# Turning the local attention's weights as two halves of 64 rows, with a PSUM bank for each half

## The chip, the cores and the metric

The kernel runs on one core of one Trainium2 chip. The metric is the device time of one execution in microseconds (us). The time before is the median of three runs, 1090.08 us (1089.24 to 1092.59).

## What is computed

Two kinds of attention are added, and the sum goes through a layer norm and a two-layer network with a residual. In the shapes of this case there are 8 batches, 8 heads, 576 positions and a head size of 64, so 4608 rows of 512 numbers reach the network, all in float32.

```python
# local attention: each position sees the 7 positions around it
mask = np.abs(pos[:, None] - pos[None, :]) < 4
scores = np.where(mask, scale * np.matmul(q, k.transpose(0, 1, 3, 2)), -1e9)
out_local = softmax(scores) @ v
# pooled attention: q, k and v averaged over groups of 4 positions
out_up = np.repeat(softmax(scale * q_d @ k_d.T) @ v_d, 4, axis=2)
x = (out_up + out_local) laid out as (8, 576, 512)
xn = (x - mean) / np.sqrt(var + 1e-6) * g_ln
return x + np.maximum(xn @ w_ch1, 0.0) @ w_ch2      # 512 -> 2048 -> 512
```

## The kernel before

**The work and its tiles.** The local attention is cut into 40 windows, five for each batch. A window holds two blocks of 64 positions and all 8 heads, so its tiles have 128 rows. The pooled attention runs in 16 halves of four heads. The network takes the 4608 rows in 18 chunks of 256 (two tiles of 128 rows each); in each chunk there are 8 steps `p` of `up` (line 940, tile `h`) and `down` (line 963, tile `acc`). Both products are made of three products of split float32 numbers, which is why TensorE carries most of the time.

**One window** (`local(i)`), in the order of its data:

- SyncE loads q and k (`qr`, `kr`, line 391: eight loads each, in two groups of four, one group for each half `jb`) and v (`vwin`, line 409, four loads). VectorE turns q and k in blocks of 32 (`lqt`, `lkt`, line 472). In the first seven windows TensorE turns them instead (line 431).
- TensorE makes the scores `ls` (line 513, 32 products of 64x64, each on a quarter of the array). VectorE masks them and subtracts the largest, ScalarE makes the exponentials `la` (line 539), a tile of 128 rows by 8 heads by 64.
- **`turn_a` (line 548) turns `la`**: four transposes of 128x128 on TensorE, one for each pair of heads, into one PSUM bank `lt`. **`turn_a_out` (line 555)** copies that bank to SBUF on ScalarE as `at`, one instruction of 128x512.
- `times_v` (line 569) multiplies by v: 32 products of 64x64 by 64x65 into two banks `lv`. It reads rows 0 to 63 of `at` for one set of products and rows 64 to 127 for the other, in all columns.
- VectorE divides (`xl`, line 585; sometimes ScalarE, line 588), and SyncE moves the rows of `xl` to the tiles `x` of the network (line 628).

**From a window to the network** (`norm(n)`): SyncE loads the pooled result `up` (line 831), GpSimd adds it to `x` (line 855), VectorE makes the statistics `st` and `mv` (line 859), GpSimd the root, VectorE the normed tile `xn` (line 869), and TensorE turns it (`px`, line 879) for the chunk that follows. Tile n needs the last of the windows that overlap it: tile 27 needs window 31, and tile 29 needs window 33.

**What sets the order.** All steps are tasks of a `Plan`. Each task names an engine, a length, the tasks that it needs, a due time, and the rooms that it takes and gives: 87 buffers in SBUF (`u`), eight PSUM banks (`a`), two staging buffers. `order()` goes through an imagined time and picks on each engine the task with the earliest due time among those that can start. That order is then the program's order on every engine, SyncE's queue of loads among them, and each engine keeps it: an instruction that waits holds all that stands behind it on its engine. A task with `alt` may go to a second engine, whichever starts sooner. So a new length or a new room of one task can move other tasks, on any engine.

Of the kernel before, what the change touches and what calls it, by code (L numbers as in the profile page):

```python
# [22 lines left out]
class Plan:  # L23
# [14 lines left out]
    def add(self, eng, dur, fn, deps=(), due=0.0, take=(), give=(), lag=None, ahead=1e9, alt=None, kb=0):  # L38

        opts = {eng: (dur, fn, 0.0)}  # L40
        if alt is not None:
            opts[alt[0]] = alt[1:]
        t = SimpleNamespace(
            n=len(self.tasks), opts=opts, dur=dur, deps=[d for d in deps if d is not None],
            due=due, take=take, give=give, lag=lag, ahead=ahead, open=0.0, waits=0, eng=None, fn=None, kb=kb,
        )
        self.tasks.append(t)
        return t
# [91 lines left out]
def attention_then_ffn(  # L140
# [10 lines left out]
    nc = tc.nc  # L151

    P = 128
# [17 lines left out]
    NPAIR = H // 2  # L171
# [15 lines left out]
    def unit(shape, name, dtype=F32, kind="u"):  # L187
        kind = kind if kind in SEP else "u"
        return work.tile(shape, dtype, tag=kind, bufs=SEP.get(kind, NU), name=name)

    def psa(name):
        return ps_a.tile([P, 512], F32, tag="a", name=name)
# [9 lines left out]
    ident = const.tile([P, P], F32, name="ident")  # L202
# [64 lines left out]
    def window_at(i):  # L267
        if NWIN <= i < NWIN + NEARLY:
            return w_base + i * w_gap - EARLY
        return w_base + i * w_gap if i >= NWIN else norm_at(0) - B0W - B0W_GAP * (2 - i)  # L270
# [21 lines left out]
    U, A, STG = (("u", 1),), (("a", 1),), (("stg", 1),)  # L292
    DMA, LAT, W_AHEAD = 0.5, 2.9, 40

    def act(n, sbuf=False):
        return (0.155 if sbuf else 0.14) + n / 1430.0

    def dve(n):
        return 0.06 + n / 950.0
# [72 lines left out]
    def window_start(w, par):  # L372
        return min(max(NQ * (2 * w + par) - (FACTOR - 1), 0), S - 64)

    last_local = SimpleNamespace(v=[None, None])

    def local(i):
        b, w = divmod(i, NWIN)
        due = window_at(i)
        add = plan.add  # L380
        x = SimpleNamespace(r={}, p={}, raw={})
# [14 lines left out]
        def load_rows(src, nm):  # L396
            x.raw[nm] = unit([P, H, D], f"{nm}n{i}")
            for par in range(2):
                t0 = window_start(w, par)
                nc.sync.dma_start(  # L400
                    x.raw[nm][64 * par : 64 * par + 64], src[b, :, t0 : t0 + 64, :].rearrange("h c d -> c h d")
                )
# [20 lines left out]
        for src, nm in ((q, "q"), (k, "k")):  # L423
            if by_pe:
# [16 lines left out]
                def sums(nm=nm):  # L441

                    for par in range(2):
# [16 lines left out]
                t = add("SP", 1.46, lambda src=src, nm=nm: load_rows(src, nm), (), due - 12.0, take=U,  # L460
                        lag=LAT, kb=256, ahead=AHEAD)
                t = add("PE", 0.43, turn, (t,), due - 8.0, take=A, give=U)
                if own:
                    t = add("DVE", 4 * dve(120), sums, [t] + gsum_done.get((b, nm), []), due - 8.0,
                            take=() if w else (("u", 2),))
# [16 lines left out]
        vt = add("SP", 4 * DMA, load_v, (last_local.v[i % 2],), due - 8.0, lag=LAT, kb=256, ahead=AHEAD)  # L482
# [35 lines left out]
        def masked(n):  # L518
            nc.vector.tensor_add(x.ps[n], x.ps[n], mask.unsqueeze(1).broadcast_to([P, NPAIR, 64]))
# [23 lines left out]
                    nc.scalar.activation(a[:, pr], x.ps[h2][:, pr], AF.Exp, scale=SCALE, bias=x.mx[:, n : n + 1])  # L543

        def turn_a():
            x.pt = psa(f"lt{i}")
            for pr in range(NPAIR):
                nc.tensor.transpose(  # L548
                    x.pt[:, pr * P : (pr + 1) * P],
                    x.a[:, 2 * pr : 2 * pr + 2].rearrange("p h j -> p (h j)"), ident,  # L550
                )

        def turn_a_out():
            x.at = unit([P, NPAIR, P], f"at{i}")
            nc.scalar.copy(x.at.rearrange("p h j -> p (h j)"), x.pt)

        def times_v():

# [14 lines left out]
        def inverse(h2):  # L573
            r = work.tile([P, NPAIR], F32, tag="lr", bufs=8, name=f"lr{i}_{h2}")
            nc.vector.tensor_scalar_add(r, x.pv[h2][:, :, D], 1e-9)
            nc.vector.reciprocal(r, r)
            x.r[h2] = r

        def divided(h2, eng):
            if h2 == 0:  # L580
                x.xl = unit([P, H, D], f"xl{i}")
            xl = x.xl.rearrange("p (c h) d -> p h c d", h=2)[:, h2]
            pv, r = x.pv[h2], x.r[h2]
            if eng == "DVE":
                nc.vector.tensor_mul(xl, pv[:, :, :D], r.unsqueeze(2).broadcast_to([P, NPAIR, D]))
                return
            for pr in range(NPAIR):
                nc.scalar.activation(xl[:, pr], pv[:, pr, :D], AF.Copy, scale=r[:, pr : pr + 1])

        by_dve = i in SHIFTED or i >= LATE  # L590
        t = add("PE", 0.75, scores_by_pair if by_pe else scores_by_block, turned, due - 6.0,
                take=(("a", 2),), give=(("u", 2),))
        if not by_pe:
            t = add("DVE", dve(256), lambda: masked(0), (t,), due - 5.0)
            t = add("DVE", dve(256), lambda: masked(1), (t,), due - 5.0)
        t = add("DVE", 2 * dve(256) + (2 * dve(256) if by_dve else 0.15), largest_by_pair, (t,), due - 5.0)
        t = add("ACT", 2 * act(256) if by_dve else 1.6, exps_by_pair, (t,), due - 5.0, take=U, give=(("a", 2),))
        t = add("PE", 0.43, turn_a, (t,), due - 3.0, take=A, give=U)
        at = add("ACT", act(512), turn_a_out, (t,), due - 3.0, take=U, give=A)
        last_local.v[i % 2] = tv = add("PE", 0.7, times_v, (at, vt), due - 1.0, take=(("a", 2),), give=U)  # L600
        outs = []
        for h2 in range(2):
            t = add("DVE", 0.28, lambda h2=h2: inverse(h2), (tv,), due)
            outs.append(
                add("DVE", dve(256), lambda h2=h2: divided(h2, "DVE"), [t] + outs, due, take=() if h2 else U, give=A,
                    alt=("ACT", 4 * act(64), lambda h2=h2: divided(h2, "ACT"), 0))
            )
        moves = []
        for par in range(2):
            s0 = NQ * (2 * w + par)  # L610
            n = min(NQ, S - s0)
            t, r0 = b * S + s0, s0 - window_start(w, par)
            while n:
                m = min(n, P - t % P)
                moves.append((t // P, t % P, r0, m, par))
                t, r0, n = t + m, r0 + m, n - m
        for e, (n, p0, r0, m, par) in enumerate(moves):

            def move(n=n, p0=p0, r0=r0, m=m, par=par):
# [7 lines left out]
                for h2 in range(2):  # L627
# [5 lines left out]
            t = add("SP", DMA if by_pe else 2 * DMA, move, outs, due + 1.0, take=() if n in piece else U,  # L633
                    give=U if e == len(moves) - 1 else (), lag=LAT, kb=116)
# [370 lines left out]
    for i in range(NPB * NWIN):  # L1005
        local(i)
    for b in range(B):
        pooled(b)
    for i in range(NPB * NWIN, B * NWIN):
        local(i)  # L1010
# [42 lines left out]
```

## Time and profile before

| | |
|---|---|
| median of three runs | 1090.08 us |
| the profiled execution's own time | 1095.81 us |
| its span, first to last instruction | 1092.7 us |
| TensorE busy (matmul) | 1040.4 us, 95% |
| VectorE, ScalarE, GpSimd busy | 504.5, 311.0, 268.8 us |
| mean granted TensorE clock | 0.973 |

The profile records one execution, so all durations come from an execution that took 5.73 us more than the median of the runs. PE is TensorE's matmul row and PEld its weight loads, DVE is VectorE, ACT ScalarE, POOL GpSimd, SP SyncE. A timeline's row gives the start in us, the time that the group of like instructions covers, the engine and line, the operation, its tiles and shapes, and how often; in brackets stands the idle time ahead of it and what ended it. Matmul rows overlap, since they are pipelined: what a group takes from the others is read from starts, not from durations. A row of the windows gives, for each engine, the busy time and in brackets the number of instructions that run in that stretch, those included that began ahead of it; then the granted clock.

### The profile page before, as it was taken

The numbers are of one execution on the slowest core, as the hardware profiler recorded it, in microseconds if no ns is written. First come the engines' busy times: TensorE is split into PE (matmuls) and PEld (weight loads), VectorE is DVE, ScalarE is ACT, GpSimd is POOL, SyncE is SP. The second block draws the span as 40 slices with busy tenths as digits, with TensorE's granted clock in tenths as the row PEclk, the third lists the DMA queues.
The fourth block names the chain that finished last, engine by engine and source line by source line (L and its number), as shares of the span: only waits on it lengthen the run. The fifth ranks groups of instructions, "written<-read, shape, count | busy, mean of one in ns | idle before, by whom it ended". The sixth has DMA issues, their size and how long they took to land.

```text
span 1092.7 us, 23624 instructions
## 1 busy us (share of the span) xinstructions
PE 1040.4 (95%) x9182; PEld 929.1 (85%) x9182; DVE 504.5 (46%) x1305; ACT 311.0 (28%) x852; POOL 268.8 (25%) x277
## 2 busy tenths in 40 slices
PE   7879889989999999999999999999988999999998
PEld 6768778878989898899898889898977989888997
DVE  7579863624344443453533443544424353543211
ACT  5366542313322222131322132223212222212100
POOL 2224556322202440041323231132400230100000
PEclk9679899999999999999999999999998999999999
DMA  7589845533433543325353534244433243320000
GB/s 147 130 227 269 214 126 125 137 75 82 103 72 80 113 101 70 90 62 122 71 119 74 123 74 113 43 113 90 116 68 76 62 98 62 81 53 29 9 20 19
DMA packets 289885, 105.38 MB, mean 96 GB/s; under 512 B 238022, under 2 KB 276166, under 8 KB 289774
## 3 DMA queue, kind: packets, MB, share of 16 engines
q1 hardware_dynamic: 289774, 103.88, 40.9%
q8 instruction: 72, 1.18, 0.5%
q14 instruction: 39, 0.32, 0.1%
HBM read 82.58 MB, written 11.80 MB: 86 GB/s over the span
## 4 chain that ended last, share of the span: by engine, by line
PE 72%; DMA 10%; SPq 7%; DVE 5%; issue 3%; POOL 3%; ACT 1%; DVEq 0%; POOLq 0%; ACTq 0%
PE h L940 30%; PE acc L963 29%; DMA x<-xl 4%; PE gv L768 2%; SPq L628 2%; PE lv L569 2%; PE gs L732 2%; PE ls L513 2%; DMA s<-in_moe_w_ch_dram 2%; DVE cva L343 1%; PE lt L548 1%; SPq L391 1%; PE px L879 1%; SPq L409 1%; PE gt L751 1%
## 5 line engine op out<-in xcount | busy, mean ns | idle before, releaser
L963 PE MATMUL acc<-hi,hl 128*128 128x512 f32 x576 | 239.5, 416 | 5.5 <-DVE hl L951 5.5
L963 PE MATMUL acc<-lo,hh 128*128 128x512 f32 x576 | 229.7, 399 | 0.0
L963 PE MATMUL acc<-hi,hh 128*128 128x512 f32 x576 | 227.6, 395 | 0.0
L947 ACT ACTIVATE hh<-h 128x512 fp32r<-128x512 f32 x144 | 86.3, 599 | 429.5 <-PE h L940 374.2
L951 DVE SCALAR_TENSOR_TENSOR hl<-h,hh 128x512 fp32r<-128x512 f32 x144 | 98.7, 685 | 216.3 <-ACT hh L947 201.4
L940 PE MATMUL h<-xh,lo 128*128 128x256 f32 x1152 | 192.9, 290 | 0.3 <-POOL lo L356 0.3
L940 PE MATMUL h<-xlo,hi 128*128 128x256 f32 x1152 | 185.6, 283 | 0.0
L940 PE MATMUL h<-xh,hi 128*128 128x256 f32 x1152 | 184.8, 283 | 0.0
L940 PEld LDWEIGHTS h<-xh,lo 128*128 128x128 f32 x1152 | 168.7, 189 | 17.7 <-POOL lo L356 0.6
L940 PEld LDWEIGHTS h<-xlo,hi 128*128 128x128 f32 x1152 | 159.0, 192 | 0.4
L940 PEld LDWEIGHTS h<-xh,hi 128*128 128x128 f32 x1152 | 158.3, 191 | 0.0
L855 POOL TENSOR_TENSOR x<-x,up 128x512 f32<-128x512 f32 x32 | 41.1, 1286 | 429.9 <-DMA x<-xl 266.5
L963 PEld LDWEIGHTS acc<-hi,hh 128*128 128x128 f32 x576 | 109.9, 191 | 25.4
L963 PEld LDWEIGHTS acc<-hi,hl 128*128 128x128 f32 x576 | 110.5, 192 | 22.6 <-DVE hl L951 6.5
L963 PEld LDWEIGHTS acc<-lo,hh 128*128 128x128 f32 x576 | 110.8, 192 | 13.0
L886 ACT ACTIVATE xh<-px,gain 128x128 fp32r<-128x128 f32 x144 | 43.6, 371 | 87.1 <-PE px L879 58.1
L859 DVE BATCH_NORM_STATS2 st<-x 128x6 f32<-128x512 f32 x36 | 24.8, 690 | 83.9 <-POOL x L855 83.8
L896 DVE SCALAR_TENSOR_TENSOR xlo<-px,gain,xh 128x128 fp32r<-128x128 f32 x144 | 42.4, 342 | 35.7 <-ACT xh L886 31.5
L343 DVE SCALAR_TENSOR_TENSOR cva<-s,cva 128x256 int32<-128x256 int32 x64 | 42.0, 697 | 1.1
L745 ACT ACTIVATE ag<-gs,gmx 96x144 f32<-96x144 f32 x96 | 29.0, 372 | 45.7 <-DVE gmx L737 42.5
L768 PEld LDWEIGHTS gv<-vd,agt 72*72 72x72 f32 x512 | 39.1, 151 | 2.4 <-POOL vd L680 0.8
L768 PE MATMUL gv<-vd,agt 72*72 72x65 f32 x512 | 40.0, 234 | 0.9 <-POOL vd L680 0.7
(176 smaller groups left out, 1101.4 us busy)
## 6 DMA issues: line engine op xcount, KB each, us to landing
s<-in_moe_w_ch_dram SPq DMA_DIRECT2D x64, 256.0 KB
vwin<-in_v_dram SPq DMA_DIRECT2D x160, 64.0 KB
out_dram<-x SPq DMA_DIRECT2D x36, 256.0 KB
qr<-in_q_dram SPq DMA_DIRECT2D x264, 32.0 KB
kr<-in_k_dram SPq DMA_DIRECT2D x264, 32.0 KB
up<-ud SPq DMA_DIRECT2D x28, 256.0 KB
x<-xl SPq DMA_DIRECT2D x66, 58.0 KB
ud<-od SPq DMA_DIRECT2D x32, 72.0 KB
```

What stands on the lines that cost most here:

```text
L343: nc.vector.scalar_tensor_tensor(out=a, in0=x.raw[i].rearrange("p (n two) -> p n two", two=2)[:, :, 0], scalar=29, in1=a, op0=ALU.logical_ ...
L513: nc.tensor.matmul(x.ps[par][64 * h2 : 64 * h2 + 64, pr], lhsT=x.qt[hs, 2 * pr + h2], rhs=x.kt[hs, 2 * pr + h2], start=True, stop=True,)
L745: nc.scalar.activation(y.a[:, c], y.ps[:, c], AF.Exp, scale=POOLED_SCALE, bias=y.mx[:, c : c + 1])
L768: nc.tensor.matmul(y.pv[:, qh, h2], lhsT=y.at[kh][:, h2, qh * GH : (qh + 1) * GH], rhs=vd[:, kh, 2 * pr + h2], start=kh == 0, stop=kh == 1,)
L855: (nc.vector if by_pe else nc.gpsimd).tensor_add(xt[n], xt[n], x.up)
L859: nc.vector.bn_stats(st, xt[n])
L886: nc.scalar.activation(xh[c][i][:, k, j * P : (j + 1) * P], pxt[n][:, kc], AF.Copy, scale=gain[:, kc : kc + 1])
L896: nc.vector.scalar_tensor_tensor(out=xlo[c][i][:, k, ts], in0=pxt[n][:, kc], scalar=gain[:, kc : kc + 1], in1=xh[c][i][:, k, ts].bitcast(F ...
L940: nc.tensor.matmul(ph[c, p][:, fi], lhsT=wt[:, kc], rhs=xx[kc // 2][:, kc % 2], start=n == 0, stop=n == 3 * KC - 1)
L947: nc.scalar.activation(hh[c, p], ph[c, p], AF.Relu)
L951: nc.vector.scalar_tensor_tensor(out=hl[c, p].rearrange("p c t -> p (c t)"), in0=ph[c, p].rearrange("p c t -> p (c t)"), scalar=0.0, in1=h ...
L963: nc.tensor.matmul(acc[c][j], lhsT=lt[:, fi, ts], rhs=rt, start=p == 0 and fi == 0 and n == 0, stop=p == NPR - 1 and fi == 1 and n == 2,)
```

## The change

The transposes of `la` are cut in two halves of 64 rows. For each pair of heads there are two transposes, of rows 0 to 63 and of rows 64 to 127, each with the fitting 64x64 corner of the identity, and each half has a PSUM bank of its own. So four transposes of 128x128 become eight with 128 columns of the stationary operand and 64 of the moving one. The copy to SBUF is cut likewise: each half's bank is copied into its 64 columns of every pair, and the plan may put each copy on ScalarE or VectorE. In the plan, `turn_a` takes two banks in place of one, its length is 0.27 in place of 0.43, and each copy gives one bank back.

```diff
         def turn_a():
-            x.pt = psa(f"lt{i}")
+
+            x.pt = [psa(f"lt{i}_{n}")[:, : NPAIR * 64].rearrange("p (c j) -> p c j", c=NPAIR) for n in range(2)]
             for pr in range(NPAIR):
-                nc.tensor.transpose(
-                    x.pt[:, pr * P : (pr + 1) * P],
-                    x.a[:, 2 * pr : 2 * pr + 2].rearrange("p h j -> p (h j)"), ident,
-                )
-
-        def turn_a_out():
-            x.at = unit([P, NPAIR, P], f"at{i}")
-            nc.scalar.copy(x.at.rearrange("p h j -> p (h j)"), x.pt)
+                for n in range(2):
+                    hs = slice(64 * n, 64 * n + 64)
+                    nc.tensor.transpose(
+                        x.pt[n][:, pr], x.a[hs, 2 * pr : 2 * pr + 2].rearrange("p h j -> p (h j)"), ident[hs, hs],
+                    )
+
+        def turn_a_out(n, copy):
+            if n == 0:
+                x.at = unit([P, NPAIR, P], f"at{i}")
+            copy(x.at[:, :, 64 * n : 64 * n + 64], x.pt[n])
...
-        t = add("PE", 0.43, turn_a, (t,), due - 3.0, take=A, give=U)
-        at = add("ACT", act(512), turn_a_out, (t,), due - 3.0, take=U, give=A)
-        last_local.v[i % 2] = tv = add("PE", 0.7, times_v, (at, vt), due - 1.0, take=(("a", 2),), give=U)
+        t = add("PE", 0.27, turn_a, (t,), due - 3.0, take=(("a", 2),), give=U)
+        at = []
+        for n in range(2):
+            at.append(add("ACT", act(256), lambda n=n: turn_a_out(n, nc.scalar.copy), [t] + at, due - 3.0,
+                          take=() if n else U, give=A,
+                          alt=("DVE", dve(256), lambda n=n: turn_a_out(n, nc.vector.tensor_copy), 0.1)))
+        last_local.v[i % 2] = tv = add("PE", 0.7, times_v, at + [vt], due - 1.0, take=(("a", 2),), give=U)
```

The lines behind the change stand three to seven higher in the changed kernel (line 940 is 947 there).

TensorE at window 23, in the middle of the program, before; the number in a name is that of the window, chunk or tile:

```order
L751 MATMUL gt10_1_0_7736<-ident_66,ag10_1_7720 72x96 x3
L751 MATMUL gt10_1_1_7742<-ident_66,ag10_1_7720 72x96 x3
L548 MATMUL lt23_7751<-ident_66,la23_7695 128x128 x4
L940 MATMUL h9_1_7705<-xh9_0_7535,lo1_3_1209 128x256 x2
L940 MATMUL h9_1_7705<-xh9_1_7547,lo1_3_1209 128x256 x2
```

The same place of the changed kernel:

```order
L758 MATMUL gt10_1_0_7891<-ident_66,ag10_1_7835 72x96 x3
L758 MATMUL gt10_1_1_7896<-ident_66,ag10_1_7835 72x96 x3
L551 MATMUL lt23_0_7900<-ident_66,la23_7790 128x64
L551 MATMUL lt23_1_7901<-ident_66,la23_7790 128x64
L551 MATMUL lt23_0_7900<-ident_66,la23_7790 128x64
L551 MATMUL lt23_1_7901<-ident_66,la23_7790 128x64
L551 MATMUL lt23_0_7900<-ident_66,la23_7790 128x64
L551 MATMUL lt23_1_7901<-ident_66,la23_7790 128x64
L551 MATMUL lt23_0_7900<-ident_66,la23_7790 128x64
L551 MATMUL lt23_1_7901<-ident_66,la23_7790 128x64
L947 MATMUL h9_1_7871<-xh9_0_7685,lo1_3_1258 128x256 x2
L947 MATMUL h9_1_7871<-xh9_1_7697,lo1_3_1258 128x256 x2
```

The four full transposes are eight halves, which alternate between the two banks; their neighbours are the same.

SyncE's queue at window 31, before: the loads of k for window 32 (`kr32`) stand between the moves of window 30 and of window 31 to tile 27 (`x27`):

```order
L666 DMA raw14v1_10011<-in_v_dram 72x4x256
L409 DMA vwin0_77<-in_v_dram 64x4x64 x4
L666 DMA raw15q0_10059<-in_q_dram 72x4x256
L628 DMA x27_10064<-xl30_10044 58x4x64 x4
L391 DMA kr32_10096<-in_k_dram 32x8x32 x4
L391 DMA qr33_10129<-in_q_dram 32x8x32 x4
L666 DMA raw15k0_10160<-in_k_dram 72x4x256
L391 DMA kr32_10096<-in_k_dram 32x8x32 x4
L391 DMA qr33_10129<-in_q_dram 32x8x32 x4
L791 DMA ud6_8953<-od13_1_10183 72x2x128
L831 DMA up27_10259<-ud6_8953 128x1x512
L409 DMA vwin1_78<-in_v_dram 64x4x64 x4
```

The same stretch of the changed kernel:

```order
L391 DMA kr32_10177<-in_k_dram 32x8x32 x4
L391 DMA qr32_10131<-in_q_dram 32x8x32 x4
L673 DMA raw14v1_10223<-in_v_dram 72x4x256
L391 DMA kr32_10177<-in_k_dram 32x8x32 x4
L409 DMA vwin0_77<-in_v_dram 64x4x64 x4
L635 DMA x27_10287<-xl30_10247 58x4x64 x4
L391 DMA qr33_10338<-in_q_dram 32x8x32 x4
L673 DMA raw15q0_10356<-in_q_dram 72x4x256
L673 DMA raw15k0_10369<-in_k_dram 72x4x256
L798 DMA ud6_9143<-od13_1_10374 72x2x128
L391 DMA qr33_10338<-in_q_dram 32x8x32 x4
L838 DMA up27_10435<-ud6_9143 128x1x512
```

All eight loads of `kr32` now stand ahead of `vwin0`, so that eight loads fewer lie between window 30's moves and `vwin1`; one load, `raw15q0`, has come in between. `ud6` is no longer right ahead of `up27`, which reads it. In both kernels window 31's moves to tile 27 (two loads of 12x4x64) follow right behind `vwin1`.

VectorE's queue at the normed tile 27, before:

```order
L859 BN_STATS st27_10344<-x27_10064 128x6
L861 BN_AGGR mv27_10346<-st27_10344 128x2
L862 TENSOR_SCALAR mv27_10346<-mv27_10346 128x1
L472 STREAM_TRANSPOSE lkt32_10371<-kr32_10096 128x512
L472 STREAM_TRANSPOSE lqt33_10373<-qr33_10129 128x512
L869 TENSOR_SCALAR xn27_10385<-x27_10064,mv27_10346 128x512
```

And of the changed kernel:

```order
L472 STREAM_TRANSPOSE lqt33_10563<-qr33_10338 128x512
L866 BN_STATS st27_10565<-x27_10287 128x6
L868 BN_AGGR mv27_10567<-st27_10565 128x2
L869 TENSOR_SCALAR mv27_10567<-mv27_10567 128x1
L903 SCALAR_TENSOR_TENSOR xlo13_0_10579<-px26_10541,gain_75,xh13_0_10570 128x128 x2
L876 TENSOR_SCALAR xn27_10593<-x27_10287,mv27_10567 128x512
```

`lkt32` no longer stands between the statistics and `xn27` (it stands 20 rows ahead of the statistics), and `lqt33` has moved ahead of the statistics. Of the 80 copies of `lt` in the changed kernel, 68 stand on ScalarE and 12 on VectorE.

## The prediction, on record ahead of the result

> **What bounds the kernel now.** The page comes first: busy times, the granted clock, the chain that ended last.
>
> ```profile
> span 1092.7 us, 23624 instructions
> PE 1040.4 (95%) x9182; PEld 929.1 (85%) x9182; DVE 504.5 (46%) x1305; ACT 311.0 (28%) x852; POOL 268.8 (25%) x277
> ...
> PEclk9679899999999999999999999999998999999999
> ...
> PE 72%; DMA 10%; SPq 7%; DVE 5%; issue 3%; POOL 3%; ACT 1%; DVEq 0%; POOLq 0%; ACTq 0%
> ```
>
> TensorE is the bound: 95% busy, 72% of the chain, at full clock but for the first quarter and one dip in the 30th slice. So a change counts here by what it adds to TensorE's row of starts, and by what it does to the few places where TensorE stands still. The dip is the largest of these after the start-up. The timeline of TensorE around it, and the windows view of the ten us that follow, show it:
>
> ```profile
> 814.06 0.39 PE L963 MATMUL acc<-hi,hh 128*128 128x512 f32 x1
> 822.83 1.09 PE L879 MATMUL px<-ident,xn 128*128 128x128 f32 x4 [8.38 <-DVE xn L869]
> ...
> 817.00:827.00 10.00, 4.17 (x18) 3.17 (x18) 4.82 (x12) 1.90 (x7) 0.13 (x1) 0.50 0.30 65
> ```
>
> TensorE stood idle for 8.38 us waiting for the normed tile 27, and its clock was 0.50 until about 827, so that the 4.2 us of work from 822.83 on lost another 2.1. This wait cost about 10.5 us. The Trainium skill, "TensorE: Matmul & The Clock Gate", Part 1, says that an idle window of some 3.4 us halves the clock; this row agrees with it.
>
> **The transposes on TensorE.** The groups by line give what is replaced, and a price for a half copy; the tile view from 260 us on gives the count and who waits for the copies.
>
> ```profile
> L548 PE MATMUL lt<-ident,la 128*128 128x128 f32 x160 | 25.1, 280 | 5.8 <-ACT la L543 4.5 <-ACT la L539 1.2
> ...
> L555 ACT COPY at<-lt 128x512 f32<-128x512 f32 x40 | 23.5, 588 | 40.4 <-PE lt L548 36.6 <-issue 2.9 <-DMA out_dram<-x 0.7
> ...
> L539 ACT ACTIVATE la<-ls 128x256 f32<-128x256 f32 x64 | 22.0, 386 | 36.9 <-DVE ls L529 36.7
> ...
> L548 PE MATMUL lt<-ident,la x120: 270/272/328, 277.8 to 1006.9; 128*128 128x128 f32 x120
> ...
>   PEld lv L569: 0.4, 1
> ```
>
> There are 40 groups of four, and 30 of them lie behind 260 us, where TensorE runs without a break and every ns of its row counts. What one group takes is read from starts, in the timeline at window 23:
>
> ```profile
> 605.35 0.60 PE L548 MATMUL lt<-ident,la 128*128 128x128 f32 x4
> ...
> 606.27 0.64 PE L940 MATMUL h<-xh,hi 128*128 128x256 f32 x4
> 606.74 0.64 PE L940 MATMUL h<-xlo,hi 128*128 128x256 f32 x4
> ```
>
> From the transposes' start to the second group of `h` are 0.92 us, and one group of four `h` takes 0.47, so the transposes cost 0.45 us.
>
> No row before has products on half the rows and all columns. The nearest are the products on a quarter of the array, `ls` and `lv`, which also leave the full array and come back to it:
>
> ```profile
> 594.41 0.39 PE L963 MATMUL acc<-lo,hh 128*128 128x512 f32 x1
> 594.64 0.39 PE L963 MATMUL acc<-hi,hh 128*128 128x512 f32 x1
> 594.96 0.69 PE L513 MATMUL ls<-lkt,lqt 64*64 64x64 f32 x32
> ...
> 596.15 0.64 PE L940 MATMUL h<-xh,hi 128*128 128x256 f32 x4
> ```
>
> One `acc` takes 0.23, so a plain successor would have started at 594.87; `ls` started at 594.96, 0.09 late. From there to the second group of `h` are 1.19, less 0.47 is 0.72. So the 32 products cost 0.81 us. The windows view of the same group says how much of that is work:
>
> ```profile
> 595.06:595.41 0.35, 0.35 (x28) 1.00 0.39 61
> 594.95:595.06 0.11, 0.11 (x5) 1.00 0.42 64
> ```
>
> Up to 595.06 there run the last `acc` and the first round of four products; in the next 0.35 us these four and 24 more, which is six rounds at 0.058 us. Eight rounds are 0.46, and 0.35 us are left for going in and out. A half transpose streams 64 columns as one `ls` does, and two halves use disjoint rows and two banks, so I take four rounds of 0.058, 0.23 us, and the same 0.35: 0.58 us. That is 0.13 more than now. From both sides: without any cost of entry the group would be cheaper (the second rival); the first weight load has 128 columns in place of 64, which may add 0.05, and a round might be 0.01 dearer. So 0.11 to 0.19 where the entry is paid.
>
> The Trainium skill, "TensorEngine Tiling (Array Packing)", Key Properties, says that a change of tiling mode drains TensorE, and it lists 64x128 as a mode of its own. Of the 64x64 mode the rows above agree, with 0.35 us a visit; of 64x128 no run here shows it.
>
> Thirty groups by 0.13 are 3.9 us. Of the ten earlier groups I count five at half, since TensorE stands still between its bursts there and hides some: 0.4. **The transposes cost 4.3 us more**, bounds 3.3 (30 by 0.11) and 6 (30 by 0.19, and some).
>
> **The copies** cost nothing. Two of 128x256 on ScalarE take 0.77 us by the row of line 539 in place of 0.588, 0.18 longer; ScalarE is 28% busy, and behind 260 us `lv` waited for `at` once, for 0.4 us, since one or two groups of network products lie between. Were that cover gone, it would be 0.18 by 30, 5.4 us. A bank is taken longer; the plan has placed it, so I price that at nothing, and a bank that comes late would show as TensorE waiting for ACT or DVE.
>
> **The order of loads around tile 27.** SyncE's timeline ahead of the long wait, and then GpSimd's and VectorE's row of tile 27:
>
> ```profile
> 777.55 3.23 SPq L391 DMA_DIRECT2D qr<-in_q_dram  x4
> 782.17 0.31 SPq L666 DMA_DIRECT2D raw14v<-in_v_dram  x1
> 783.87 2.68 SPq L409 DMA_DIRECT2D vwin<-in_v_dram  x4
> ...
> 794.14 3.05 SPq L391 DMA_DIRECT2D kr<-in_k_dram  x4
> ...
> 799.67 3.08 SPq L391 DMA_DIRECT2D kr<-in_k_dram  x4
> ...
> 805.16 0.31 SPq L791 DMA_DIRECT2D ud<-od  x1
> 807.32 0.59 SPq L831 DMA_DIRECT2D up<-ud  x1
> 808.01 2.73 SPq L409 DMA_DIRECT2D vwin<-in_v_dram  x4
> 810.84 1.76 SPq L628 DMA_DIRECT2D x<-xl  x2
> ...
> 814.10 1.26 POOL L855 TENSOR_TENSOR x<-x,up 128x512 f32<-128x512 f32 x1 [26.46 <-DMA x<-xl]
> ...
> 820.57 0.71 DVE L472 STREAM_TRANSPOSE lkt<-kr 128x512 f32<-128x512 f32 x1 [4.07 <-DMA x<-xl]
> ```
>
> Window 31's product with v and its tile 29 counterpart, window 33's, give the scale:
>
> ```profile
> 800.46 0.70 PE L569 MATMUL lv<-vwin,at 64*64 64x65 f32 x32
> ...
> 870.44 1.77 SPq L628 DMA_DIRECT2D x<-xl  x2
> ...
> 880.77 0.66 PE L879 MATMUL px<-ident,xn 128*128 128x128 f32 x4 [0.48 <-DVE xn L869]
> ```
>
> Window 31 was through TensorE at about 801.1, but SyncE came to `vwin` only at 808.01: it had a backlog. Then `lkt32` held VectorE for 4.07 us more. The change moves both. The eight loads of `kr32` (3.05 + 3.08 us) go to where SyncE stood idle (780.78 to 782.17 and 782.48 to 783.87, 2.8 us); so 2.8 to 6.1 us of the backlog go. `up27` no longer waits for `ud6` (805.47 to 807.32, 1.8 us). `raw15q` comes in, 0.4. So `x27`'s last move starts 4.2 to 7.5 us sooner, at 803.3 to 806.6 (not ahead of 803, when window 31 is divided). For tile 29 the turn came 10.3 us behind that move (870.44 to 880.77), so tile 27 would be turned at 813.6 to 816.9, where TensorE wanted it at 814.3. 8.4 us of wait become 0 to 2.6, and with so short a wait I expect no half clock: 7.9 to 10.5 us less in the profiled execution. That execution took 1095.81 us and the median run 1090.08; the 5.73 us between lie in waits rather than in matmuls, part of them probably here. So for the median I take 6, bounds 2 and 10.5. What is late next: the same chain at tiles 11, 19 and 29, with waits like the 0.48 above. At window 11 eight loads have moved ahead and its tile may wait up to 1.5 us; that lies in the bounds.
>
> **The sum.** Against the profiled execution: 1095.81 + 4.3 - 9 = 1091.1. Against the median of the runs: 1090.08 + 4.3 - 6 = **1088.4 us**; its own range is 1082.9 (+3.3, -10.5) to 1094.1 (+6, -2). About 0.3%, 3.3 us, is what a measurement can tell from no change, so this forecast is "the same", chance 0.50.
>
> **The rivals.**
>
> *The wait at tile 27 stays, slower.* `kr32` asks for a buffer earlier than before, one that TensorE must set free. If it isn't free by about 784, SyncE stands there and all behind it comes as late as now; likewise `lqt33`, now ahead of the statistics, may wait for its buffer as `lkt32` did. It decides from the point at which the last move to `x27` starts later than 808: then the wait exceeds 3.5 us and the half clock is back. For it: SyncE's waits for buffers in these rows. Against it: the plan thought the buffer free. 1090.08 + 4.3 = 1094.4. Chance 0.24.
>
> *Entry costs nothing for halves.* If the array takes 64-row products beside full ones without emptying, the group is four rounds of 0.058 and some 0.05 at the end, 0.28, so 0.17 less by 30, 5.1 us gained: 1079.0 without the wait at tile 27, 1085.0 with it. For it: one column set, all 128 columns stay in use, unlike in `ls`. Against it: the 0.35 us at every visit of `ls`. Chance 0.17.
>
> *The halves don't run at once.* Then eight rounds and 0.35, 0.81 us, 0.36 more by 30: 10.8 us. 1094.9 without the wait at tile 27, 1100.9 with it. Against it: the four products of a round of `ls` start together. Chance 0.09.
>
> **How the numbers follow.** The range of 1081 to 1097 us leaves out the second rival's lower end and the third's upper end, some 2 in 10. Faster by over 0.3%: a third of the forecast (0.17) and nearly all of the second rival (0.16), 0.33. Slower: two thirds of the first rival (0.16), two thirds of the third (0.06) and a little of the forecast (0.03), 0.25. The rest, 0.42, is within 0.3%.
>
> **What would show it.** In the changed trace the eight halves should take 0.58 us by starts, with 0.09 us lost on entry and a longer first `h` or `acc` behind; 0.28 would be the second rival, 0.81 the third. `x<-xl` of tile 27 should be issued within 5 us of window 31's `lv`, and `px` of tile 27 wait under 3 us, with the clock at 1.00; a wait of over 5 us is the first rival. Wrong altogether would be a wait of TensorE for `at` or for a bank at many windows.

## The result, and the profile after

The changed kernel takes 1107.45 us (median of four runs, 1106.74 to 1108.94) against 1090.14 for the kernel before beside it: 1.0157 times as long, 95% interval 1.0137 to 1.0177. The forecast was 1088.4, at most 1097.

The page of the changed kernel shows no new bound: TensorE is busy for the same share of the span (95%), the clock row has more digits below 9 in its first half, and the late dip has stayed (the 8 among the last ten digits). Its span is 1104.8 us, its own time 1106.74.

```profile
PE 1048.1 (95%) x9342; PEld 927.3 (84%) x9342; DVE 507.6 (46%) x1320; ACT 311.0 (28%) x880; POOL 263.5 (24%) x274
...
PEclk9689899989989999999999999999998999999999
```

The groups by line say where TensorE stands. First the kernel before, then the changed one:

```profile
L879 PE MATMUL px<-ident,xn 128*128 128x128 f32 x144 | 23.1, 287 | 11.9 <-DVE xn L869 11.9
```

```profile
L572 PE MATMUL lv<-vwin,at 64*64 64x65 f32 x1280 | 29.1, 228 | 0.3 <-ACT ag L752 0.3
...
L886 PE MATMUL px<-ident,xn 128*128 128x128 f32 x144 | 24.7, 300 | 20.1 <-DVE xn L876 20.1
```

TensorE waits 20.1 us for normed tiles in place of 11.9, and 0.3 us ahead of `lv`, none of it for `at`: the two copies show no cost, and from 260 us on TensorE waits ahead of none of `lt`, `lv` and `ls`, so for no bank either. The timeline puts the new wait at tile 9 (first row) and shows that the wait at tile 27 is still there:

```profile
312.47 1.09 PE L886 MATMUL px<-ident,xn 128*128 128x128 f32 x4 [4.98 <-DVE xn L876]
...
833.01 1.11 PE L886 MATMUL px<-ident,xn 128*128 128x128 f32 x4 [5.09 <-DVE xn L876]
```

The windows view of the stretches around their ends:

```profile
310.50:317.10 6.60, 4.63 (x16) 3.89 (x17) 4.11 (x11) 2.60 (x9) 0.00 (x0) 0.50 0.31 72
...
832.80:839.40 6.60, 6.09 (x44) 4.66 (x48) 3.25 (x10) 3.61 (x13) 0.00 (x0) 0.50 0.48 115
```

At each of the two 6.6 us run at half clock (0.50); at tile 9 the first 2 of them still lie in the wait. Before, tile 9 was turned without a wait and tile 27 after 8.38 us. What goes ahead of tile 9 stands in the queues of SyncE and VectorE. SyncE in the changed kernel:

```profile
287.51 2.93 SPq L391 DMA_DIRECT2D qr<-in_q_dram  x4
...
291.41 1.87 SPq L391 DMA_DIRECT2D qr<-in_q_dram  x4
293.38 0.36 SPq L798 DMA_DIRECT2D ud<-od  x1
297.34 0.58 SPq L838 DMA_DIRECT2D up<-ud  x1
...
300.84 6.50 SPq L635 DMA_DIRECT2D x<-xl  x6
```

The same place in a second profile of the kernel before:

```profile
288.09 0.37 SPq L791 DMA_DIRECT2D ud<-od  x1
292.37 0.59 SPq L831 DMA_DIRECT2D up<-ud  x1
...
295.87 6.08 SPq L628 DMA_DIRECT2D x<-xl  x6
```

VectorE there, at the first step behind window 11's product with v:

```profile
291.83 0.16 DVE L575 TENSOR_SCALAR lr<-lv 128x4 f32<-128x4 f32 x1 [5.33 <-PE lv L569]
```

And VectorE in the changed kernel:

```profile
294.20 0.16 DVE L578 TENSOR_SCALAR lr<-lv 128x4 f32<-128x4 f32 x1 [4.06 <-PE lv L572]
...
310.95 0.71 DVE L472 STREAM_TRANSPOSE lqt<-qr 128x512 f32<-128x512 f32 x1 [3.90 <-DMA x<-xl]
311.77 0.55 DVE L876 TENSOR_SCALAR xn<-x,mv 128x512 f32<-128x512 f32 x1
```

The eight loads of `qr13` now stand ahead of `ud2`. The store `ud2` goes out at 293.38 in place of 288.09 (2.4 of these 5.3 us were there already, by the rows of VectorE: 294.20 and 291.83). Its reload `up9` can follow only 4.0 us later, and SyncE stands there, with `vwin` and window 11's moves behind. They start 6.6 us after window 11's product (294.20), before 4.0 (295.87 behind 291.83). Then VectorE stands 3.90 us at `lqt13`, which needs a buffer that those moves give back, and `xn9` is queued behind it. So tile 9 is late twice from one cause.

### The profile page after: what moved, and what is told of

The parts are those of the page before. It is cut to its first block, busy times and chain, and to the rows that moved or that the text cites. A ratio compares the mean times of both kernels' runs of the same rounds, so it can differ in the third digit from the quotient of the medians.

```text
span 1104.8 us, 24051 instructions
## 1 busy us (share of the span) xinstructions
PE 1048.1 (95%) x9342; PEld 927.3 (84%) x9342; DVE 507.6 (46%) x1320; ACT 311.0 (28%) x880; POOL 263.5 (24%) x274
## 4 chain that ended last, share of the span: by engine, by line
PE 75%; DMA 11%; SPq 7%; DVE 4%; issue 2%; ACT 1%; POOL 0%; DVEq 0%; POOLq 0%; ACTq 0%
PE h L947 31%; PE acc L970 31%; DMA s<-in_moe_w_ch_dram 4%; DMA x<-xl 3%; PE gv L775 3%; PE lv L572 2%; PE gs L739 2%; SPq L635 2%; PE ls L513 2%; PE gt L758 1%; SPq L391 1%; PE lt L551 1%; SPq L400 1%; PE px L886 1%; DMA raw2q<-in_q_dram 1%
## 5 line engine op out<-in xcount | busy, mean ns | idle before, releaser
L970 PE MATMUL acc<-hi,hl 128*128 128x512 f32 x576 | 240.3, 417 | 11.0 <-DVE hl L958 10.9
L886 PE MATMUL px<-ident,xn 128*128 128x128 f32 x144 | 24.7, 300 | 20.1 <-DVE xn L876 20.1
```

The costliest lines, as they stand in the source:

```text
L886: nc.tensor.transpose(pxt[n][:, kc], xn[n][:, kc * P : (kc + 1) * P], ident)
L970: nc.tensor.matmul(acc[c][j], lhsT=lt[:, fi, ts], rhs=rt, start=p == 0 and fi == 0 and n == 0, stop=p == NPR - 1 and fi == 1 and n == 2,)
```

## The experiments

Ratios are to the kernel before, run beside each; 1% is 10.9 us.

**The kernel before again.** No edit.

> The kernel before, unchanged, profiled and timed again: the yardstick for the rest. Both theories expect 1089 to 1092 us. What it is for is the profile: the profiled execution of before took 5.7 us more than the median of its runs. If that excess was the wait of 8.4 us at tile 27 with its half clock, this profile shows tile 27 with a wait under 4 us and a span of 1085 to 1088 us; if the wait belongs to every execution of this order, it is 8 to 9 us again and the span about 1087 to 1093 us, and the excess lies elsewhere.

1089.69 us, ratio 1.0000 (0.9989 to 1.0012). Tile 9's transposes in the profile that the prediction used (tile 27's start at 822.83 there), then tile 9's and tile 27's in this one:

```profile
310.83 0.60 PE L879 MATMUL px<-ident,xn 128*128 128x128 f32 x4
```

```profile
304.90 0.60 PE L879 MATMUL px<-ident,xn 128*128 128x128 f32 x4
...
816.74 1.09 PE L879 MATMUL px<-ident,xn 128*128 128x128 f32 x4 [7.05 <-DVE xn L869]
```

The wait at tile 27 belongs to the order: it is there in an execution of 1089.67 us as well. The excess of the first profile is elsewhere: of 6.1 us at tile 27, 5.9 are there by tile 9, in the start-up.

**Halves in the old order, full transposes in the new one, a new order alone.** The first edit puts the halves in the plan of before, with one task for both copies, so that nearly all stands where it stood:

```diff
-        t = add("PE", 0.43, turn_a, (t,), due - 3.0, take=A, give=U)
-        at = add("ACT", act(512), turn_a_out, (t,), due - 3.0, take=U, give=A)
+        t = add("PE", 0.43, turn_a, (t,), due - 3.0, take=(("a", 2),), give=U)
+        at = add("ACT", act(512), turn_a_out, (t,), due - 3.0, take=U, give=(("a", 2),))
```

> The eight halves into two banks, in the order of the kernel before: length 0.43 as before, one task on ScalarE for both copies, so that six of SyncE's rows and three of TensorE's differ from before. Theory one (the halves cost 0.11 to 0.15 us a group by themselves, and the rest of the 17 us is the plan's new order of loads and of VectorE's work): 1094.5 to 1096.5 us. Theory two (the halves cost all of it, directly or by what they delay): 1105 to 1109 us. Theory three (the second bank and the split copies cost it, since products wait for a bank or for the later copy): 1100 to 1106 us, with waits of TensorE ahead of lt, lv or ls at many windows.

The second keeps all numbers of the changed plan and turns in full (the added lines):

```diff
+            x.pt = [psa(f"lt{i}_{n}")[:, : NPAIR * 64].rearrange("p (c j) -> p c j", c=2) for n in range(2)]
             for pr in range(NPAIR):
...
+                nc.tensor.transpose(
+                    x.pt[pr // 2][:, pr % 2], x.a[:, 2 * pr : 2 * pr + 2].rearrange("p h j -> p (h j)"), ident,
+                )
...
+            copy(x.at[:, 2 * n : 2 * n + 2], x.pt[n])
```

> The changed kernel's plan, number for number, so its order on every engine, its two banks and its two copies; but four full transposes of 128x128, two pairs of heads into each bank, in place of the eight halves. Theory one (the order costs most): 1101 to 1103.5 us, the changed kernel less 4 to 6. Theory two (the halves cost all): 1089 to 1091 us. Theory three (banks and copies): 1101 to 1106 us, with waits ahead of lt, lv or ls rather than ahead of px.

The third is the kernel before with one number changed:

```diff
-        t = add("PE", 0.43, turn_a, (t,), due - 3.0, take=A, give=U)
+        t = add("PE", 0.27, turn_a, (t,), due - 3.0, take=A, give=U)
```

> The kernel before with one number changed: the plan thinks that the transposes take 0.27 us in place of 0.43. Full transposes, one bank, one copy; 158 of SyncE's 1179 instructions stand elsewhere than before. Theory one (the order of loads decides where tiles wait, and a small shift of the plan can add or take several us): 2 us or more off before in either direction, below 1088 or above 1092, and waits ahead of px at other tiles than before. Theories two and three: within 1.5 us of before, 1088.6 to 1091.6 us.

Halves in the old order: 1102.23 us, 1.0114 (1.0095 to 1.0134), between theories one and two. It lies in the range of theory three, but without its sign: from 140 us on, TensorE waited 3.2 us ahead of `lt` and 1.1 ahead of `lv`, where it waited 5.5 and 1.4 in the second profile of before. Full transposes in the new order: 1099.61, 1.0084 (1.0065 to 1.0103), a little under theory one. The length alone: 1102.35, 1.0121 (1.0102 to 1.0140). The new order without halves costs 9 us, and a number in the plan, with not one instruction on TensorE dearer, costs 12, so theory two cannot be the whole story. The timeline of the run with the length alone has tile 9's wait with the same neighbours on SyncE:

```profile
292.54 2.93 SPq L391 DMA_DIRECT2D qr<-in_q_dram  x4
296.49 0.38 SPq L791 DMA_DIRECT2D ud<-od  x1
296.93 1.87 SPq L391 DMA_DIRECT2D qr<-in_q_dram  x4
301.21 0.59 SPq L831 DMA_DIRECT2D up<-ud  x1
```

And on TensorE:

```profile
315.64 1.12 PE L879 MATMUL px<-ident,xn 128*128 128x128 f32 x4 [7.35 <-DVE xn L869]
```

The 12 us of the run with halves in the old order were not yet the halves' own. Its order had still changed in the start-up, where VectorE waited for the conversion of a weight, and TensorE for VectorE. VectorE in that run:

```profile
123.07 0.95 DVE L340 TENSOR_SCALAR cva<-cva 128x512 int32<-128x512 int32 x1 [5.93 <-ACT cva L332]
```

Here the waits of TensorE from 120 to 135 us, in that run and then in the second profile of before:

```profile
PE acc L966 <- DVE hl L954: 7.9, 1, 7.9
```

```profile
PE acc L963 <- DVE hl L951: 3.8, 2, 3.1
```

**Halves in exactly the old order, once and twice.** Windows 0 to 6 keep full transposes, so every other instruction stands where it stood, on all engines (the copies are cut and take two banks for the same windows):

```diff
+            if i >= 7:
+                return turn_halves()
```

> The eight halves in two banks for windows 7 to 39, four full transposes for windows 0 to 6; every other instruction stands where it stands before, on every engine. Theory one (the halves cost 0.145 us a group and nothing else; the 12 us of the halves in the old order had 6 in the start-up, where that kernel's order had still changed): 33 groups by 0.145 are 4.8 us, so 1094 to 1097 us with up to 2 more at the tiles that wait. Theory two (the halves delay everything behind them and cost 12 us in any order): 1101 to 1103 us.

```diff
+            for pr in list(range(NPAIR)) * 2:
```

> As the run before, but each half is turned twice (16 products a group in place of eight, the second eight writing the same values again). If a group is one fixed cost for leaving and entering the full array and 0.058 us for each round of two halves, a group takes 0.58 + 0.23 = 0.81 us, and the time is 7.7 us over the run before, about 1103 us. If the price lies in each half by itself (0.58 / 8 = 0.073 us), a group takes 1.16 us and the time is 19 us over the run before.

1097.45 us, 1.0057 (1.0037 to 1.0077), so 6.2 us, interval 4.0 to 8.4: theory one, though 0.5 us above its range, with 4.8 from the groups themselves. Twice: 1100.58, 1.0089 (1.0055 to 1.0123). One group in each timeline, once and twice:

```profile
572.54 0.64 PE L955 MATMUL h<-xlo,hi 128*128 128x256 f32 x4
573.11 0.46 PE L550 MATMUL lt<-ident,la 64*128 64x64 f32 x8
...
574.08 0.64 PE L955 MATMUL h<-xh,hi 128*128 128x256 f32 x4
```

```profile
575.28 0.64 PE L955 MATMUL h<-xlo,hi 128*128 128x256 f32 x4
575.85 0.71 PE L550 MATMUL lt<-ident,la 64*128 64x64 f32 x16
...
577.07 0.64 PE L955 MATMUL h<-xh,hi 128*128 128x256 f32 x4
```

From the `h` ahead to the second `h` behind are 1.54 and 1.79 us. Less two groups of `h` at 0.48, the eight halves take 0.58 and the sixteen 0.83: four rounds cost 0.25, so a round 0.0625, and 0.33 us are fixed, paid once a visit. The Trainium skill, "TensorEngine Tiling (Array Packing)", Key Properties, says that changing the tiling mode drains TensorE; these rows, with 0.33 us a visit, agree for the mode of 64 rows by 128 columns. The doubled run adds 33 by 0.25, 8.3 us of work, and only 3 us of time, where 7.7 were expected. The intervals leave some -1 to 8 us for that difference; the 19 us of a price in each half are out. A likely reason is that TensorE comes later to tiles that it would have waited for anyway: in the two profiles it waits 12.9 us ahead of `px` once and 10.2 twice, at tile 27 alone 6.99 and 5.45. No run shows it for the rest.

**One tile first on VectorE.** The order is solved as before, then tasks, found by name, are put behind another:

```diff
+        tasks = plan.order()
+        for late, first in (('lqt33', 'xn27'), ('lkt32', 'xn27')):
+            late, first = named[late], named[first]
+            tasks.remove(late)
+            tasks.insert(tasks.index(first) + 1, late)
```

> The kernel before with one move: on VectorE the normed tile 27 is made ahead of the transposes of k for window 32 and of q for window 33, which waited 4.1 us there for a buffer. Theory one (such a transpose, standing between the statistics and the normed tile and waiting for a buffer that a window's moves give back, is what makes TensorE wait): the wait at tile 27 falls from 7.2 to 8.5 us to 3 to 4.5, the half clock behind it from 10.2 us to 3.4 to 6.8, and the time to 1082.5 to 1086 us, under both kernels. Rival (the time is bound by the late moves to tile 27 or by what stands behind the transposes, so the wait moves on): 1088.5 to 1091 us.

In the changed kernel the same for `lqt13` and `xn9`; a memset on GpSimd awaits the buffer in VectorE's place.

> The changed kernel with one move: on VectorE the normed tile 9 is made ahead of the transpose of q for window 13, and the buffer that this transpose waits for is awaited on GpSimd, by a memset of one column that is written over. Theory one (VectorE's stand at that transpose, 3.9 us, is the larger part of the wait at tile 9): the wait at tile 9 falls from 5.3 to about 1.2 us, its half clock of 6.8 us goes to 0 to 3.4, and the time from 1107.5 to 1100 to 1102 us. Rival (the later moves of window 11 set it, or the wait passes to the next tiles): 1105.5 to 1108 us.

1088.55 us, 0.9969 (0.9951 to 0.9987), and 1104.76, 1.0131 (1.0108 to 1.0154). The first lies in its rival's range, the second 0.7 us under it. The waits of TensorE at tile 27 and behind it, in the first:

```profile
812.94 0.66 PE L881 MATMUL px<-ident,xn 128*128 128x128 f32 x4 [2.42 <-DVE xn L871]
...
818.59 1.75 PE L734 MATMUL gs<-ktg,qbdg 128*96 128x144 f32 x6 [2.68 <-DVE hl L954]
```

At tile 9, in the second:

```profile
307.95 0.66 PE L896 MATMUL px<-ident,xn 128*128 128x128 f32 x4 [0.98 <-DVE xn L886]
...
314.92 0.98 PE L749 MATMUL gs<-ktg,qbdg 128*96 128x144 f32 x6 [3.22 <-ACT ktg L735]
```

The wait for the tile fell as expected, and a wait ahead of `gs` took its place, since another instruction still stood for a buffer that the moves give back: in the first run ScalarE's `xh` for the chunk of tiles 26 and 27, in the second the memset on GpSimd, with VectorE's `lqt13` behind it:

```profile
815.68 1.14 ACT L888 ACTIVATE xh<-px,gain 128x128 fp32r<-128x128 f32 x4 [11.94 <-DMA x<-xl]
```

```profile
310.64 0.10 POOL L474 MEMSET lqt<- 128x1 f32 x1 [3.33 <-DMA x<-xl]
```

So the moves themselves had to come sooner.

**The loads back behind the moves.** Window 13's loads of q, in the changed kernel, go behind window 11's moves; window 33's, in the kernel before, behind window 31's. The loop is the one above, with these pairs:

```diff
+        for late, first in (('qr13_1', 'moves11'), ('qr13_0', 'moves11'), ('lqt13', 'lkt13')):
...
+        for late, first in (('qr33_1', 'moves31'), ('qr33_0', 'moves31'), ('lqt33', 'lkt33'), ('lkt32', 'xn27')):
```

> The changed kernel with window 11's place on SyncE as it was before: the eight loads of q for window 13 go behind window 11's moves, and VectorE's transpose of them behind that of k for window 13. Theory one (these loads, now ahead of the store and reload of the pooled result and so of the moves, make tile 9 late, and the buffers that the moves give back late too): the moves start 3 to 3.5 us sooner against window 11's product with v (lag 3 to 3.7 us in place of 6.6), the wait at tile 9 falls from 5.3 us to under 1, no wait of 3 us takes its place, and the time falls from 1107.5 to 1099 to 1102 us. Rival (the wait only moves on, as when tile 9 alone was put first on VectorE): 1104 to 1107 us.

> The same cure for the kernel before, at window 31: the eight loads of q for window 33 go behind window 31's moves, VectorE's transpose of them behind that of k for window 33, and the transpose of k for window 32 behind the normed tile 27. Theory one: the moves start 3 to 4 us sooner, the wait at tile 27 falls from 7 to 8.5 us to 1 to 4, no wait of 2.7 us ahead of gs takes its place, and the time is 1082.5 to 1086 us, below both kernels. Rival (another wait takes its place): 1087.5 to 1091 us.

The changed kernel: 1096.19 us, 1.0058 (1.0041 to 1.0076). Eight loads in another place give back 10.8 us, two to three more than the most that was expected. The two profiles put less of it at the edit: of the 12.0 us between them 2.6 lie ahead of window 11's product, where the same instructions stand, and 6.2 between that product and window 12's. SyncE at window 11, and then TensorE at tile 9:

```profile
287.59 0.37 SPq L802 DMA_DIRECT2D ud<-od  x1
292.13 0.58 SPq L842 DMA_DIRECT2D up<-ud  x1
...
295.50 6.07 SPq L638 DMA_DIRECT2D x<-xl  x6
```

```profile
305.89 0.63 PE L890 MATMUL px<-ident,xn 128*128 128x128 f32 x4 [1.02 <-DVE xn L880]
```

The kernel before: 1081.73 us, 0.9921 (0.9897 to 0.9945), 8.6 us less than the faster of the two kernels takes, and 0.8 under the expected range. Moves on VectorE alone gave 3.4 us in the run above. In its timeline tile 27 is turned without a wait:

```profile
812.40 0.60 PE L883 MATMUL px<-ident,xn 128*128 128x128 f32 x4
```

**True numbers in the plan.** The plan counts 1.0 us for two moves of a window; the rows of `x<-xl` above show 6.1 to 6.5 us for six. It counts 0.27 for the halves; they take 0.58.

```diff
-            t = add("SP", DMA if by_pe else 2 * DMA, move, outs, due + 1.0, take=() if n in piece else U,
+            t = add("SP", DMA if by_pe else 4 * DMA, move, outs, due + 1.0, take=() if n in piece else U,
```

> The kernel before with one number of the plan set to what the trace shows: two moves of a window to a tile take SyncE 2.0 us in place of 1.0. Nothing else is edited, but 210 of SyncE's 1179 instructions then stand elsewhere. Theory one in its narrow form (wrong lengths in the plan cause the late moves): 1080 to 1088 us. Its wide form (the old order is one that came out well, and any other order of this plan pays for waits at other tiles, as the shorter length alone did with 12 us): 1094 to 1108 us. If the order did not matter: 1089 to 1091 us.

```diff
-        t = add("PE", 0.27, turn_a, (t,), due - 3.0, take=(("a", 2),), give=U)
+        t = add("PE", 0.58, turn_a, (t,), due - 3.0, take=(("a", 2),), give=U)
```

> The changed kernel with the plan's length of the halves set to what they take, 0.58 us in place of 0.27; 124 of SyncE's instructions stand elsewhere than in the changed kernel. Theory that the wrong length makes the order bad: 1098 to 1102 us, the old order's time with halves and little more. Wide form of theory one (any new order pays): 1102 to 1112 us, with waits at other tiles than in the changed kernel.

Both edits in the changed kernel:

> The changed kernel with two of the plan's numbers set to what the traces show: 2.0 us for two moves of a window to a tile and 0.58 for the halves. If true numbers are what makes an order good, it comes to the time of the kernel before with true moves plus the halves' price for 40 groups, 1077.9 + 5.8 to 8, so 1083.5 to 1086 us. If that order was one good draw among others, anything up to 1100 us.

1077.89 us, 0.9888 (0.9862 to 0.9915), the fastest of all and 2 us under its expectation, though TensorE still waits 6.37 us at tile 9 in its profile; 1099.69, 1.0090 (1.0067 to 1.0113); 1089.11, 0.9976 (0.9960 to 0.9991). Each truer plan was faster than the one that it replaced, by 12, 7 and 20 us. But the last missed its expectation by 3 us, and nothing here gave these sizes in advance: "any new order pays" is as wrong as "true numbers give the best order".

**Does it add up?** Full transposes with window 11's loads put back, and halves in the order of the true moves (windows 7 to 35, all else exactly as there):

> The changed kernel's plan with window 11's loads of q put back behind the moves, and full transposes in place of the halves. If the 17 us are the halves' own price and the place of those loads, and the two add up, both are gone here: 1096.2 less 4.8 to 6.6, so 1089.5 to 1091.5 us, the time of the kernel before. If the rest of the new order still costs something, 1092 to 1096 us; if the halves cost nothing in this order, 1096.

> The kernel before with the plan's true length for the moves, and the eight halves in two banks for windows 7 to 35 in place of the full transposes; all other instructions stand as in the run with the true moves (1077.9 us). 29 groups by 0.145 are 4.2 us, and by what the halves cost in the old order (6.6 us for 33 groups) 5.8: 1082 to 1084 us if the price does not depend on the order. If tiles that wait soak it up or add to it, outside of 1081 to 1085.

1095.28 us, 1.0033 (1.0013 to 1.0052), and 1081.76, 0.9916 (0.9895 to 0.9937). In us against before, by the ratios:

| order | full | halves | difference |
|---|---|---|---|
| before (halves in windows 7 to 39) | 0 | +6.2 | 6.2 |
| the change's | +9.2 | +17.1 | 7.9 |
| the change's, loads back at 11 | +3.6 | +6.3 | 2.7 |
| true moves (windows 7 to 35) | -12.2 | -9.2 | 3.0 |

Each difference is uncertain by 2 to 4 us, so one price of some 5 us fits all four rows. They do not add up to before: 3.6 us of the new order stay with full transposes and the loads put back. The place of the loads is worth 10.8 us with halves and 5.6 with full transposes. The profiles, one of each kernel, do not bear that difference out: from window 11's product with v to window 12's, the loads put back save 6.2 us with halves and 7.8 with full transposes.

The profiles also say where the changed kernel loses against the second profile of before. From window 11's product to window 12's (tile 9) it takes 41.26 us in place of 33.04, from window 15's to window 16's (tile 13) 31.11 in place of 26.76, and from window 31's to window 32's (tile 27) 39.74 in place of 41.98. That is 8.2 and 4.4 us lost and 2.2 gained; the other 7.4 of 17.7 us are spread over the program, the halves' 4.8 among them. Tile 13 is a second place that the new order made late. There VectorE stands at a transpose of q ahead of the statistics, and TensorE waits 3.23 us in place of 0.90, then runs at half clock (0.50) until about 436.6:

```profile
428.92 0.71 DVE L472 STREAM_TRANSPOSE lqt<-qr 128x512 f32<-128x512 f32 x1 [4.59 <-DMA raw9k<-in_k_dram]
```

```profile
433.37 1.11 PE L886 MATMUL px<-ident,xn 128*128 128x128 f32 x4 [3.23 <-DVE xn L876]
```

With window 11's loads put back and full transposes, the same stretch still takes 30.43 us, 3.7 more than before. No run changed what stands there, so its cause is not shown.

## Why the prediction was wrong

**The halves' price was right.** 0.58 us a group was forecast and 0.58 measured, with the 0.09 on entry (573.11 where a plain successor of 572.54 would start at 573.02). The fixed 0.35 and 0.058 a round were 0.33 and 0.0625. The rivals "entry costs nothing" (0.28) and "not at once" (0.81) are out. In time it was 6.2 us for 33 groups where the order was kept, just above the upper bound of 6.

**Copies and banks were right:** no wait for `at`.

**The step that failed is "At window 11 eight loads have moved ahead and its tile may wait up to 1.5 us".** The tile waited 4.98 us, with half clock up to 317.1, and putting the loads back gave 10.8 us. The prediction gives no working for the 1.5 us. It did not ask what the loads were moved past: the store `ud2`, whose reload 4.0 us later holds SyncE; and it left out that the buffers given back by the moves are awaited on VectorE ahead of `xn`. The prediction's own rows of tile 27 showed both (a stand from 805.47 to 807.32 for `ud6`, 4.07 us for `lkt32`). Tile 13, with its 4.4 us, is not among the tiles that it named as late next (11, 19 and 29).

**The gain at tile 27 came in part.** "8.4 us of wait become 0 to 2.6", it said; 5.09 stayed, with 6.6 us at half clock. The term "`up27` no longer waits for `ud6`" failed. Window 31's product and SyncE in the changed kernel:

```profile
813.59 0.70 PE L572 MATMUL lv<-vwin,at 64*64 64x65 f32 x32
```

```profile
809.38 3.03 SPq L391 DMA_DIRECT2D qr<-in_q_dram  x4
...
813.42 0.38 SPq L798 DMA_DIRECT2D ud<-od  x1
813.85 1.89 SPq L391 DMA_DIRECT2D qr<-in_q_dram  x4
818.26 0.57 SPq L838 DMA_DIRECT2D up<-ud  x1
...
822.11 6.18 SPq L635 DMA_DIRECT2D x<-xl  x6
```

`kr32` had left this place, but `qr33` was still in it and the store went out late, so SyncE stood from 815.74 to 818.26. The moves started 8.5 us after the start of window 31's product in place of 10.4 (800.46 to 810.84): 1.9 us sooner, where 4.2 to 7.5 were forecast. On VectorE `lkt32` had gone from its place, and another instruction waited 4.18 us for a buffer:

```profile
831.89 0.61 DVE L903 SCALAR_TENSOR_TENSOR xlo<-px,gain,xh 128x128 fp32r<-128x128 f32 x2 [4.18 <-DMA x<-xl]
```

What the wait is worth was sized rightly: 9 us forecast, 8.6 gained where it went. But the discount from 9 to 6 for the median rested on "part of them probably here", and the profile's excess was in the start-up.

**The rivals.** "The wait at tile 27 stays" was right about tile 27 by its own sign, a wait of over 5 us. Its 1094.4 us is still 13 too few, since no rival had tile 9 or tile 13. A plan that is solved anew can move loads at all 40 windows; the prediction worked it out only where before waited longest, and there a new order can hardly lose.

## What to carry over

When a change re-solves an order, read every place where the old one had little slack, not only the one where it waited, and follow each moved transfer to what it is moved past: a store with its reload behind it held SyncE's whole queue for some 4 us here. Keep the order and make the edit alone to price it, and change a number of the plan alone to price the order; here the two were 6 and 9 to 12 us. And a wait that was removed by moving its instruction alone came back behind it, both times, until what was waited for came sooner.

## What was not expected of the hardware

The same wait can cost half clock or none. Ahead of tile 13 TensorE waited 2.23 us in the run with halves in the old order and 2.29 in the run that kept the order exactly; the windows view of the next 3.3 us, first and second run:

```profile
427.60:430.90 3.30, 3.30 (x12) 2.62 (x11) 3.30 (x11) 2.18 (x9) 0.00 (x0) 0.50 0.29 46
```

```profile
423.30:426.60 3.30, 3.30 (x20) 2.61 (x18) 3.30 (x11) 2.46 (x9) 0.00 (x0) 1.00 0.36 57
```

The clock is 0.50 in one and 1.00 in the other, though in both TensorE had run without a break at 1.00 ahead of the wait. So the prediction's "with so short a wait I expect no half clock" does not always hold. The Trainium skill, "TensorE: Matmul & The Clock Gate", Part 1, says that the clock is judged in windows of some 3.4 us that run freely, and that it is halved after an idle one. These two rows agree with it only in part: a wait of 2.23 us cannot fill such a window, and the clock fell all the same. Where a wait falls in a window may decide; no run here shows that.
